# A recurrent attention with an MoE layer: wide products on four tiles, turns by transposes, slabs of two chunks, and an order that counts TensorE's recent use

## The chip, the cores and the metric

The kernel runs on one core of one Trainium2 chip. The core has five engines that each work through their own queue of instructions in order: TensorE (PE in the profile, with its weight loads as PEld), VectorE (DVE), ScalarE (ACT), GpSimd (POOL) and SyncE (SP). DMAs are issued from the queues of ScalarE and SyncE. The metric is the device time of one execution in microseconds (us), as a median of several runs.

## The reference

For each of 4 x 8 heads a 40 x 40 state runs over 768 steps, and its output then goes through a layer norm and a two-layer product with a relu.

```python
for t in range(S):
    y[:, :, t] = np.einsum('bhd,bhde->bhe', rt, state)
    Sa = np.einsum('bhde,bhe->bhd', state, at)
    state_decay = state * wt[:, :, None, :] - np.einsum('bhd,bhe->bhde', Sa, bt)
    state = state_decay + np.einsum('bhd,bhe->bhde', vt, kt)
...
xn = (x - mu) / np.sqrt(var + 1e-06) * g_ln
ch = np.maximum(xn @ w_ch1, 0.0) @ w_ch2
return (x + ch).astype(np.float32)
```

x is y with the heads side by side, so 320 wide; w_ch1 is 320 x 1280 and w_ch2 1280 x 320.

## The kernel before

The 768 steps are cut into 24 chunks of 32. Inside a chunk the recurrence becomes products of matrices, for all 32 heads at once, and only the state passes from chunk to chunk. The heads are laid out by four bits: `h2` and `j`, `gg`, and two bits `b`. Sixteen blocks (`P`) lie along the free dimension and two halves of 40 partitions (rows 0 to 39 and 64 to 103; `half`) or four quarters of 32 (`quad`) along the partitions.

What runs for each chunk c:

- `prep`: ScalarE's queue loads w, a and kb. VectorE makes running products of the decay (`g`, L431, and `q`, L440) and GpSimd scales a and kb by them. TensorE then makes the products of kb with a (`pg`, L477, 64 x 32 results), which VectorE multiplies by a mask of signs into `gk`; the transposes `KB` of kb (L498) and `gY` of g (L464). SP stores half of `gk` to DRAM (`dg`).
- `invert`: for a slab of several chunks, SP fetches the 16 x 16 diagonal blocks from DRAM (`yl`), VectorE inverts them in 14 steps of two instructions for the whole slab (L367, tiles `y` and `tmpy`), and SP writes the result to DRAM twice (`td`, L540, and `ta`, L543). `SLABS` lists the slabs: two of two chunks, then five of four.
- `chain`: the part that goes from chunk to chunk. SP loads N, A and T back from DRAM. `j1` and `j2` (L576) complete the inverse. `pra` and `prb` (L550) add, in one PSUM tile, the share of the chunk's own v (`vpart`) and of the state (`spart`). `p3` (L627) makes u, ScalarE copies it into `VU` beside v (L634), `ST` (L649) is the change of the state, and VectorE adds it.
- `post`: `S` (L685) and `uT` (L699) turn the state and u by products with the identity, `pz` (L710) makes scores, VectorE masks them into Z, and `y` (L550) sums Z with KB and r with S.
- `norm` and `moe`: layer norm of the result, its transposes (L844, L846), and for each pair of chunks 20 units of MoE work: ten of eight products of the first layer (`ph`, L883 and L887) and ten of six of the second (`po`, L903), with a relu on ScalarE (L891) and the remainder on VectorE (L894) between.

A product's place in the array follows from the partitions of its operands: rows of the array from where the two inputs lie, columns from where the output lies. In `pg_` and `pz_` the input half and the output half are the same index (`half(h2)` and `half(h2, 64)`), in `s_` and `sp_` they are two different ones.

The order of all queues is fixed when the program is built. `Plan.order` is a simulation in the kernel's own code: each step has an engine, a planned duration, a key (smaller goes first) and what it depends on, and at each moment each engine takes the ready step with the smallest key. Two things concern TensorE. First, the planner keeps a model of its clock: in windows of `WIN` us it adds up planned time times `FILL`, a share of the array that it gives to each kind of step, and the next window is planned at full or half speed by that sum. Second, MoE units fill in: a unit is taken at once where none was for `DENSE` = 2.0 us; otherwise they are held back (`PACE`) if few are left for the work that is to come. Where TensorE has nothing ready between 25 and 500 us of the plan (`WARM`), it gets a step `wz` of two products (L972) of a constant tile, whose result nobody reads. `BASE` holds the first key of each family of steps.

## Time and profile before

| | |
|---|---|
| median of 3 runs | 950.91 us |
| lowest and highest | 950.14 and 967.42 us |
| the profiled execution | 950.51 us, of which its span is 948.8 |
| PE busy, of the span | 816.7 us, 86% |
| PE weight loads busy | 744.9 us |
| DVE, ACT, POOL busy | 344.3, 199.1, 155.7 us |
| mean granted clock of TensorE | 0.723 |
| DMA moved | 73.85 MB |

The span runs from the first instruction to the last; the time of an execution lies 1.7 us above it here. A row of the lines view names a line, an engine, the tiles written and read, and how often the instruction stands; behind the bar are its busy time in us and the mean of one in ns, then the idle time of the engine just before, and what ended it. A row of the timeline has a start and a duration in us. A row of the windows view is a stretch of the span: its length, the busy time of each engine with the number of instructions, the granted clock, the DMA share and the rate in GB/s; for a single line only PE and PEld stand there. A float32 product is two instructions of the trace, so the 32 of a group in the program are 64 in the profile; a transpose and an MoE product are one.

### The profile page before, as it was taken

To read this page: it belongs to the slowest core of one execution; us is meant where nothing else is said; L and a number is where in the kernel's file an instruction comes from. 1 tells how busy PE (TensorE), PEld (TensorE's weight loads), DVE (VectorE), ACT (ScalarE), POOL (GpSimd) and SP (SyncE) were. 2 spreads that over 40 slices of the span, in tenths; PEclk is the share of its full clock that TensorE was granted. 3 is DMA by queue.
4 is the path that set the end of the run, shared out by engine and by line. 5 is a ranking of instruction groups with operands and counts; after the bars stand their busy time and mean duration, and the time that the engine had idled before them with its cause. 6 is when DMAs were issued, how large, how long until landed. Compare 5 with 4: busy or idle time off the path is not lost. (4 is left out here: it accounts for less than half of the span.)

```text
span 948.8 us, 44592 instructions
## 1 busy us (share of the span) xinstructions
PE 816.7 (86%) x20924; PEld 744.9 (79%) x20924; DVE 344.3 (36%) x700; ACT 199.1 (21%) x433; POOL 155.7 (16%) x215
## 2 busy tenths in 40 slices
PE   3779999999698999699999598999688999678997
PEld 3678988988687888588888587888688889577797
DVE  5374234589202238401227511217711225012231
ACT  1042334421111122111212021212112211112211
POOL 4151123363200003300004300003300000000000
PEclk9985556699655569655659776558866969678799
DMA  8764434344412224622133532124332131211000
GB/s 209 182 154 105 114 89 99 95 119 91 106 46 70 47 67 89 134 53 52 42 78 99 107 85 51 44 62 114 69 75 49 44 65 21 63 41 35 18 2 31
DMA packets 164182, 73.85 MB, mean 78 GB/s; under 512 B 131352, under 2 KB 146712, under 8 KB 163992
## 3 DMA queue, kind: packets, MB, share of 16 engines
q10 hardware_dynamic: 59256, 50.22, 21.1%
q1 hardware_dynamic: 104736, 20.72, 11.0%
q8 instruction: 165, 2.70, 1.2%
q14 instruction: 25, 0.20, 0.1%
HBM read 59.64 MB, written 11.27 MB: 75 GB/s over the span
## 5 line engine op out<-in xcount | busy, mean ns | idle before, releaser
L903 PE MATMUL po<-w_f,hh 128*128 128x320 f32 x480 | 135.5, 372 | 1.0 <-issue 1.0
L883 PE MATMUL ph<-xh,w_f 128*128 128x256 f32 x480 | 135.4, 341 | 0.0
L883 PEld LDWEIGHTS ph<-xh,w_f 128*128 128x128 f32 x480 | 99.6, 229 | 4.6 <-issue 1.0
L903 PEld LDWEIGHTS po<-w_f,hh 128*128 128x128 f32 x480 | 93.7, 227 | 4.4 <-issue 1.3
L894 DVE SCALAR_TENSOR_TENSOR hl<-ph,hh 128x512 fp32r<-128x512 f32 x60 | 41.0, 684 | 149.5 <-ACT hh L891 149.5
L903 PE MATMUL po<-w_f,hl 128*128 128x320 f32 x240 | 85.2, 355 | 0.8 <-DVE hl L894 0.8
L710 PEld LDWEIGHTS att<-r,vt 40*64 40x64 f32 x1536 | 75.3, 200 | 6.7 <-issue 5.6
L367 POOL TENSOR_TENSOR a<-a,g 104x512 f32<-104x512 f32 x24 | 31.6, 1316 | 298.4 <-DVE g L431 177.9
L710 PE MATMUL att<-r,vt 40*64 40x32 f32 x1536 | 78.6, 274 | 2.2 <-issue 2.2
L883 PE MATMUL ph<-xl,w_f 128*128 128x256 f32 x240 | 77.3, 322 | 0.0
L477 PE MATMUL att<-a,kb 40*64 40x32 f32 x1536 | 57.4, 235 | 16.8 <-POOL kb L367 8.1
L972 PE MATMUL po<-warm 128*128 128x192 f32 x346 | 71.2, 372 | 0.0
L477 PEld LDWEIGHTS att<-a,kb 40*64 40x64 f32 x1536 | 54.7, 153 | 20.5 <-POOL kb L367 9.3
L972 PEld LDWEIGHTS po<-warm 128*128 128x128 f32 x346 | 63.5, 277 | 2.2
L367 DVE TENSOR_TENSOR Z<-att,mask 128x512 f32<-128x512 f32 x24 | 16.6, 690 | 134.2 <-PE att L710 78.7
L891 ACT ACTIVATE hh<-ph 128x512 fp32r<-128x512 f32 x60 | 35.9, 598 | 124.7 <-PE ph L887 118.6
L576 PE MATMUL att<-A,N 16*32 16x16 f32 x1536 | 25.3, 204 | 42.3 <-DMA A<-d_a 38.3
L367 POOL TENSOR_TENSOR kb<-kb,q 104x1024 f32<-104x1024 f32 x22 | 54.4, 2472 | 25.8 <-issue 19.2
L634 ACT COPY VU<-att 32x320 f32<-32x320 f32 x96 | 40.0, 417 | 85.4 <-PE att L627 81.0
L576 PEld LDWEIGHTS att<-A,N 16*32 16x32 f32 x1536 | 22.9, 141 | 43.6 <-DMA A<-d_a 31.6
L903 PEld LDWEIGHTS po<-w_f,hl 128*128 128x128 f32 x240 | 54.9, 229 | 2.4 <-DVE hl L894 1.3
L865 POOL TENSOR_SCALAR sm<-mv 128x2 f32<-128x2 f32 x12 | 4.7, 388 | 316.6 <-DVE mv L837 316.5
(114 smaller groups left out, 1334.7 us busy)
## 6 DMA issues: line engine op xcount, KB each, us to landing
w<-in_w_dram ACTq DMA_DIRECT2D x24, 416.0 KB
kb<-in_kb_dram ACTq DMA_DIRECT2D x24, 416.0 KB
a<-in_a_dram ACTq DMA_DIRECT2D x24, 208.0 KB
r<-in_r_dram ACTq DMA_DIRECT2D x24, 208.0 KB
vt<-in_dv_dram ACTq DMA_DIRECT2D x24, 208.0 KB
VU<-in_vt_dram ACTq DMA_DIRECT2D x48, 80.0 KB
VS<-in_vs_dram ACTq DMA_DIRECT2D x48, 80.0 KB
out_dram<-ot SPq DMA_DIRECT2D x24, 160.0 KB
```

Of the source, the lines that this page charges most:

```text
L367: eng.tensor_tensor(out=out, in0=a, in1=b, op=op)
L477: M.matmul(banks(o)[half(h2, 64), b // 2, C * (4 * (b % 2) + 2 * gg + j):C * (4 * (b % 2) + 2 * gg + j) + C], lhsT=kb[half(h2), 2 * (4 * j ...
L576: M.matmul(bank(o)[quad(b), 16 * x:16 * x + 16], lhsT=lhsT[quad(b, n), x], rhs=rhs(b, x), start=True, stop=True, skip_group_check=True)
L634: lambda o, qs=qs, gg=gg, cb=cb, p3=p3: COPY(out=VU[qs].rearrange("p (x y n) d -> p x y n d", x=2, y=2)[:, :, cb], in_=banks(p3)[qs, :, 0: ...
L710: M.matmul(bank(o)[half(gg, 64), C * x:C * x + C], lhsT=flat(vt.rearrange("p n x t -> p n (x t)"))[half(gg), 64 * x:64 * x + 64], rhs=r[ha ...
L865: G.tensor_scalar(out=sm[:, 2], in0=mv[:, :, 1], scalar1=1e-6, scalar2=None, op0=ALU.add)
L883: M.matmul(pv, lhsT=l, rhs=r[:, k], start=n == 0, stop=False, skip_group_check=True)
L891: A.activation(out=hh, in_=ph, func=AF.Relu)
L894: V.scalar_tensor_tensor(out=hl, in0=ph, scalar=0.0, in1=hh.bitcast(F32), op0=ALU.max, op1=ALU.subtract)
L903: M.matmul(po[u][:, 0:CH], lhsT=l[:, us], rhs=wt[:, y], start=f == 0 and n == 0, stop=f == 9 and n == 2, skip_group_check=True)
L972: M.matmul(po_t[0][:, CH:512], lhsT=warm_t[:, 0:128], rhs=warm_t, start=False, stop=True, skip_group_check=True)
```

## The change

Five things change.

1. `pg_` and `pz_` give the output half and the input half different indices, so that a chunk's 32 products use all four combinations. Where results lie in PSUM changes with it: `gk` becomes [128, 4, 4, 32], its sign product two instructions, Z becomes [128, 2, 8, 32], and r and dv are laid out otherwise by the host.
2. `S` and `uT` become transposes of two neighbouring blocks at once: 16 instead of 32 products in the program. For that the blocks of `VU` and `ST` are padded from 40 to 64 columns, and GpSimd clears the four tiles once.
3. `vpart` reads v from `VU`; the tile `VS` and its two loads a chunk go. Its products are split in two by whether their input rows and their bank go together. Between the halves a new step `fence` writes one element of each bank on VectorE. y is split likewise: half of r with S (`ys`), a fence, Z with KB and the other half of r with S (`yz`).
4. All slabs have two chunks.
5. The planner counts use: `used(t)` is planned clock times fill over the last `WIN` us. Where it is below `LOW` = 0.46, TensorE takes an MoE unit if one is ready, otherwise a step `wz`, now a single product of 512 columns into a free ph tile. `DENSE` and `PACE` go. Keys in `BASE`, several planned durations and `FILL` change.

```diff
-SLABS = [[0, 1], [2, 3]] + [list(range(i, i + 4)) for i in range(4, NCH, 4)]
+SLABS = [[i, i + 1] for i in range(0, NCH, 2)]
...
-BASE = dict(chain=-100.0, post=-60.0, prep=-70.0, inv=-45.0, load=-90.0, moe=400.0, wts=-20.0)
+BASE = dict(chain=-48.0, post=-64.0, prep=-66.0, inv=-53.0, load=-90.0, moe=94.0, wts=-20.0)
...
-WIN, DENSE, PACE = 3.413, 2.0, 0.7
-WARM = 25.0, 500.0
+WIN, LOW, WARM = 3.413, 0.46, 20.0
...
+        def used(t):
+
+            while hist and hist[0][1] <= t - WIN:
+                hist.pop(0)
+            return sum((b - max(a, t - WIN)) * f for a, b, f in hist) / WIN
...
-                        if now and t - dense > DENSE:
+                    if e == "PE" and t >= WARM and moes and used(t) < LOW:
...
+        for n in range(RING["VU"]):
+            add("zVU", "POOL", 0.2, lambda o, n=n: G.memset(VU_t[n], 0.0), -890, writes=[("zVU", n)])
...
-                        M.matmul(banks(o)[half(h2, 64), b // 2, C * (4 * (b % 2) + 2 * gg + j):C * (4 * (b % 2) + 2 * gg + j) + C],
+                        M.matmul(banks(o)[half(gg, 64), h2, C * bj:C * bj + C],
                                  lhsT=kb[half(h2), 2 * (4 * j + b) + gg],
...
+    def fence(name, first, key):
+
+        add(name, "DVE", 0.1, lambda o: V.memset(banks(first)[0:1, :, 511:512], 0.0), key, frm=first)
...
-            add(f"ld_s{c}_{gg}", "ACT", 0, lambda o, gg=gg: A.dma_start(
-                out=flat(VS)[quad(2 * gg)], in_=vs_in[c, gg]), kl, writes=[("VS", c, gg)], nbytes=82000)
...
+        def vpart(t, same):
+            for j in range(2):
+                for b in range(4):
+                    for gg in range(2):
+                        h2 = gg if same else 1 - gg
+                        n, y = 8 * (b % 2) + 4 * (b // 2) + 2 * h2 + j, 2 * j + gg
+                        acc_mm(t[quad(b), h2, D * y:D * y + D], seen, (b, h2), gk[quad(2 * gg), b, 2 * h2 + j],
+                               VU[quad(2 * gg), n, 0:D])
...
+        fence(f"prf{c}", pr, k - .1)
+
+        def prb(o):
+            vpart(banks(pr), True)
+            if c:
+                spart(banks(pr))
...
-                            M.matmul(banks(o)[half(gg), h2, D * jb:D * jb + D], lhsT=ST[half(h2), 8 * gg + 2 * b + j],
-                                     rhs=ident[half(h2), half(h2)], start=True, stop=True, skip_group_check=True)
+                        M.transpose(out=banks(o)[0:104, h2, D * gb:D * gb + D],
+                                    in_=flat(ST)[half(h2), 128 * gb:128 * gb + 104],
+                                    identity=ident[half(h2), half(h2)])
...
-                    M.matmul(bank(o)[half(gg, 64), C * x:C * x + C],
-                             lhsT=flat(vt.rearrange("p n x t -> p n (x t)"))[half(gg), 64 * x:64 * x + 64],
-                             rhs=r[half(gg), x], start=True, stop=True, skip_group_check=True)
+                        M.matmul(banks(o)[half(gg, 64), j, C * bh:C * bh + C], lhsT=flat(vt.rearrange("p n x t -> p n (x t)"))[half(j), 64 * n:64 * n + 64],
+                                 rhs=r[half(j), n], start=True, stop=True, skip_group_check=True)
...
+            py = add(f"ys{c}", "PE", 0.28, lambda o: ys(()), k + .45, reads=[("r", c), ("S", c)], nb=2, mode=(64, 32))
+            fence(f"yf{c}", py, k + .55)
...
-        for n in range(2):
-            M.matmul(po_t[0][:, CH:512], lhsT=warm_t[:, 0:128], rhs=warm_t, start=False, stop=True,
-                     skip_group_check=True)
+        w = fin["w1_0_0"] if o.late[1] else hh_t[0]
+        M.matmul(ph_t[o.late[0]], lhsT=w[:, 0:128], rhs=w, start=True, stop=True, skip_group_check=True)
```

Counted over the whole program, the steps `wz` are 346 products before and 74 after, and the fences 47. What that makes of the order is shown at three places. In the rows, "x32" is the number of equal instructions of the program in a row, att are the two PSUM tiles of the attention, and the numbers behind a name tell buffers apart.

The first place is TensorE's queue early on, where the first two chunks are worked through. Before:

```order
L649 MATMUL att_69<-VU_117,KB_105 40x40 x32
L710 MATMUL att_70<-r_122,vt_120 64x32 x32
L699 MATMUL att_70<-ident,VU_117 40x32 x32
L972 MATMUL po_73<-warm 128x192 x10
L550 MATMUL att_69<-VS_118,gk_100 32x40 x32
L550 MATMUL att_69<-ST_135,a_89 32x40 x32
L550 MATMUL att_70<-KB_104,Z_138 32x40 x32
L972 MATMUL po_73<-warm 128x192 x2
L685 MATMUL att_69<-ident,ST_136 40x40 x32
```

And after, at the same steps:

```order
L721 MATMUL att_70<-r_119,vt_117 64x32 x32
L691 MATMUL att_69<-ident,ST_133 104x40 x16
L998 MATMUL ph_71<-hh_155 128x512
L549 MATMUL att_70<-KB_103,Z_135 32x40 x32
L549 MATMUL att_69<-VU_116,gk_98 32x40 x16
L998 MATMUL ph_71<-hh_155 128x512
L474 MATMUL att_70<-a_90,kb_92 64x32 x32
L549 MATMUL att_69<-VU_116,gk_98 32x40 x16
L549 MATMUL att_69<-ST_133,a_87 32x40 x32
```

The turn of the state is 16 instructions of 104 columns instead of 32 of 40, the products of gk with v come in two halves of 16 with another group between them, and single wide `wz` products stand where runs of narrow ones did.

The second place is VectorE's queue near the end of the inversion of the second slab. Before:

```order
L367 TENSOR_TENSOR tmpy<-y_133 128x26
L367 TENSOR_TENSOR y_133<-y_133,tmpy 128x13x2
L367 TENSOR_TENSOR tmpy<-y_133 128x14
L367 TENSOR_TENSOR y_133<-y_133,tmpy 128x14
L536 COPY yT_131<-y_133 128x16x16
```

After, at the end of the same inversion:

```order
L360 TENSOR_TENSOR y_130<-y_130,tmpy 128x13x2
L360 TENSOR_TENSOR xt_137<-att_70,pi_109 128x2x4x40
L862 BN_STATS st_147<-xt_137 128x6
L863 BN_AGGR mv_149<-st_147 128x2
L866 TENSOR_SCALAR xc_142<-xt_137,mv_149 128x320
L554 MEMSET att_69 1x2
L360 TENSOR_TENSOR tmpy<-y_130 128x14
L360 TENSOR_TENSOR y_130<-y_130,tmpy 128x14
L535 COPY yT_128<-y_130 128x16x16
```

The fence (L554) stands in the same queue as the steps of the inversion and of the layer norm, and comes when these are done.

The third place is TensorE's queue in the middle of the run, where MoE units and attention groups alternate. Before, one second-layer unit (L903, six products) and what stands around it:

```order
L649 MATMUL att_69<-VU_117,KB_105 40x40 x32
L903 MATMUL po_73<-w_3_f,hh_159 128x320 x2
L903 MATMUL po_73<-w_3_f,hl_161 128x320
L903 MATMUL po_74<-w_3_f,hh_159 128x320 x2
L903 MATMUL po_74<-w_3_f,hl_161 128x320
L576 MATMUL att_70<-T_125,W_130 32x16 x32
L699 MATMUL att_70<-ident,VU_117 40x32 x32
L550 MATMUL att_69<-VS_118,gk_100 32x40 x32
L550 MATMUL att_69<-ST_135,a_89 32x40 x32
```

After, two such units (L929):

```order
L929 MATMUL po_73<-w_6_f,hh_156 128x320 x2
L929 MATMUL po_73<-w_6_f,hl_158 128x320
L929 MATMUL po_74<-w_6_f,hh_156 128x320 x2
L929 MATMUL po_74<-w_6_f,hl_158 128x320
L707 MATMUL att_69<-ident,VU_115 104x32 x16
L657 MATMUL att_70<-VU_115,KB_103 40x40 x32
L929 MATMUL po_73<-w_7_f,hh_156 128x320 x2
L929 MATMUL po_73<-w_7_f,hl_158 128x320
L929 MATMUL po_74<-w_7_f,hh_156 128x320 x2
L929 MATMUL po_74<-w_7_f,hl_158 128x320
L721 MATMUL att_69<-r_119,vt_117 64x32 x32
L549 MATMUL att_70<-VU_116,gk_98 32x40 x16
```

Four attention groups stood between this unit and the next; now it is two.

## The prediction

> **What bounds the kernel now.** I read the page's busy rows and its clock row first, then the cores view for the mean granted clock.

> ```profile
> span 948.8 us, 44592 instructions
> PE 816.7 (86%) x20924; PEld 744.9 (79%) x20924; DVE 344.3 (36%) x700; ACT 199.1 (21%) x433; POOL 155.7 (16%) x215
> PEclk9985556699655569655659776558866969678799
> q1 hardware_dynamic: 104736, 20.72, 11.0%
> ```
> ```profile
> core 0: 948.8 us, clock 0.723
> ```

> TensorE is busy 86% of the span and nothing else reaches 40%, so TensorE sets the time. But its clock is granted at 0.723 on average. It has two values here, 0.50 and 1.00, so (1 - 0.723) / 0.5 = 55% of the span, 526 us, ran at half. The windows view says where.

> ```profile
> 75.00:100.00 25.00, 24.52 (x520) 22.91 (x522) 9.75 (x32) 5.52 (x13) 3.22 (x4) 0.50 0.44 107
> 300.00:325.00 25.00, 23.75 (x736) 20.71 (x738) 5.35 (x10) 4.74 (x10) 0.40 (x1) 0.50 0.19 45
> 400.00:425.00 25.00, 23.08 (x689) 21.01 (x684) 1.51 (x2) 5.52 (x15) 1.28 (x1) 0.50 0.25 64
> ```
> ```profile
> 300.00:325.00 25.00, 0.00 (x0) 0.00 (x0) 0.50 0.19 45
> 400.00:425.00 25.00, 5.90 (x18) 4.70 (x18) 0.50 0.25 64
> 650.00:675.00 25.00, 7.14 (x44) 6.59 (x45) 1.00 0.43 102
> ```

> The first fence is all of TensorE: busy 23 to 24.5 of 25 us, and yet at half clock. The second is the second-layer MoE products alone (L903): none in 300 to 325, 18 in 400 to 425 (half clock both times), 44 in 650 to 675, where the clock is full throughout. So "busy" is not what earns the clock. The small attention products fill little of the array; the clock comes with MoE products standing close together. In the three half-clock rows PE is busy 71.35 of 75 us, 95%, so about 526 x 0.95 = 500 of the 817 busy us, 61%, ran at half. What the half clock costs, and what the changed products cost, is in the timeline and the lines view (duration is the second column of the timeline, busy total the first number after the bar of a line).

> ```profile
> 324.82 3.63 PE L710 MATMUL att<-r,vt 40*64 40x32 f32 x64
> 736.67 2.06 PE L710 MATMUL att<-r,vt 40*64 40x32 f32 x64
> 284.47 2.34 PE L699 MATMUL att<-ident,VU 32*40 32x32 f32 x64
> 750.12 1.41 PE L699 MATMUL att<-ident,VU 32*40 32x32 f32 x64
> 739.79 0.83 PE L649 MATMUL att<-VU,KB 64*40 64x40 f32 x64
> 524.57 0.69 PE L498 MATMUL att<-ident,kb 40*128 40x40 f32 x16 [1.22 <-DVE gk L367]
> ```
> ```profile
> L710 PE MATMUL att<-r,vt 40*64 40x32 f32 x1536 | 78.6, 274 | 2.2 <-issue 2.2
> L972 PE MATMUL po<-warm 128*128 128x192 f32 x346 | 71.2, 372 | 0.0
> L477 PE MATMUL att<-a,kb 40*64 40x32 f32 x1536 | 57.4, 235 | 16.8 <-POOL kb L367 8.1 <-DMA d_g<-gk 4.7 <-POOL rec L367 3.4
> L699 PE MATMUL att<-ident,VU 32*40 32x32 f32 x1536 | 47.3, 227 | 2.1 <-issue 1.8 <-ACT xh L850 0.2
> L685 PE MATMUL att<-ident,ST 40*40 40x40 f32 x1472 | 27.8, 243 | 5.7 <-issue 5.7
> L498 PE MATMUL att<-ident,kb 40*128 40x40 f32 x384 | 19.3, 254 | 3.3 <-DVE gk L367 3.3
> ```

> The same 64 products take 3.63 us at half and 2.06 at full, 2.34 and 1.41: a us of half-clock work costs 0.57 to 0.60 us at full, so 0.40 of it can be won.

> **The sum, against the profiled execution** (950.51 us: span 948.8 and 1.7 around it; the median of the runs shown, 950.91, is 0.4 above). Of the span PE works 816.7 and is idle 132.1.

> *Wide products on four tiles (pg, L477; pz, L710).* Before, row half and column half are always equal, so two of the four 64x64 tiles work. L649 has the same 64 instructions on all four tiles and takes 0.83, where L699, on two, takes 1.41: a factor of 0.59, although each L649 streams 40 columns instead of 32. Ends: a factor of 1 (64-column weight loads don't overlap) and 0.50. I take 0.55, next to the measured 0.59: 0.45 x (78.6 + 57.4) = 61 us off; ends 0 and 68.

> *State and u by transposes.* Two-pass products with the identity become one-pass transposes, two blocks at a time: 64 instructions become 16, of the shape that L498 has, 19.3 / 24 = 0.80 us a chunk at this clock mix. L699: 47.3 - 19.3 = 28 off. L685: 27.8 - 23 x 0.80 = 9 off. Ends: 0.69 each (all at full) and about 1.1 (all at half): 31 to 43 in sum, 37 taken.

> *Warm-up products.* 346 of 192 columns, 71.2 us, become 74 of 512. At 71.2 / 66,432 columns x 37,888 columns that is 41 us; at full clock, by the L710 ratio, some 0.7 of that or less. They stand almost all ahead of the first MoE product, where TensorE waits for loads anyway. I take 24, so 47 off; ends 30 and 55.

> *Split accumulations.* The prediction product (pra, prb) and y each get one or two more switches between groups: some 0.1 us, three a chunk, 7 us more (0 to 15).

> At an unchanged clock, PE work is 816.7 - 61 - 37 - 47 + 7 = 679.

> *The order.* I laid full-clock durations of such rows on the two orders, from the first MoE product to the last. Before, 189 of 312 us of attention products stand in stretches over 2.5 us without a MoE product, the longest 6.6; after, 80 of 262, the longest 3.7. That is 61% and 31%. Before, 61% of PE's busy time is at half. I let the half share follow the stretches: of 679 us, 414 at half becomes 210, and 204 us turned to full win 0.40 x 204 = 82. This is the weakest step. Its ends: nothing won, and all 414 turned, 166. PE work: 597.

> *Slabs of two.* Each slab's inverse goes through SP's queue.

> ```profile
> 49.97 2.08 SPq L540 DMA_DIRECT2D d_t<-y  x4
> 52.14 2.03 SPq L543 DMA_DIRECT2D d_a<-yT  x4
> 64.18 0.73 PE L576 MATMUL att<-A,N 16*32 16x16 f32 x64
> 376.48 4.13 SPq L540 DMA_DIRECT2D d_t<-y  x8
> 380.71 5.34 SPq L543 DMA_DIRECT2D d_a<-yT  x8
> 395.18 1.05 PE L576 MATMUL att<-A,N 16*32 16x16 f32 x64 [6.93 <-DMA A<-d_a]
> ```
> ```profile
> PE att L576 <- DMA A<-d_a: 38.3, 5, 9.0
> ```
> ```profile
> L367 DVE TENSOR_TENSOR tmpy<-y 128x28 f32<-128x28 f32 (+13 forms) x98 | 28.5, 291 | 24.5 <-DMA y<-d_g 17.0 <-issue 4.6
> L367 DVE TENSOR_TENSOR y<-y,tmpy 128x28 f32<-128x28 f32 (+13 forms) x98 | 24.8, 253 | 3.4
> L431 DVE TENSOR_TENSOR_SCAN g<-w,start 104x512 f32<-104x512 f32 x24 | 32.8, 1368 | 2.1 <-POOL rec L367 0.8 <-PE att L464 0.6
> ```

> From the first store to the first product that needs it: 14.2 us for two chunks, 18.7 for four. SP issues 8 stores instead of 16 before a load can go. Four-chunk slabs stalled PE five times, 38.3 us. Twelve slabs now; the faster TensorE reaches the product sooner, the chain is shorter. I take 2.5 us each, 30 us; ends 0 and 12 x 7.7 = 92. VectorE gets 336 steps for 196; at 0.19 to 0.29 each that is some 25 us more, the split sign product some 5: 375 of 740 us, no bound. SP gets no more issues per chunk.

> *Fences.* 47 one-element writes on VectorE stand between two halves of an accumulation: TensorE's second half, and all behind it in its queue, waits for VectorE to reach them. In the order one group (0.4 to 2 us) mostly stands between the halves and covers a free VectorE. Ends: 0, and 47 x 1.37 behind a scan each, 64. I take 0.3 each, 14, because VectorE is busy half the time.

> *Loads.* The vs loads go (48 of 80 KB). The VU loads come in pieces of 160 bytes, 24,576 packets more; by the q1 row, the queue with the small packets, one takes 0.11 x 16 x 948.8 / 104,736 us = 16 ns, so 25 us on each of 16 engines: hidden. Four POOL memsets stand ahead of chunk 0's product, 0 to 5 us once; taken as 0.

> Idle: 132.1 - 38.3 + 30 + 14 = 138. Time: 597 + 138 + 1.7 = 737 us.

> [...] In the trace, identity transposes (L498) run in stretches that also hold MoE products, so no row tells what they earn alone. [...]

> **Rivals.**
> 1. *Full clock from the first MoE product on.* For it: the row 650 to 675, and the even order. Against it: the order is fixed, and the row 400 to 425 shows interleaved MoE products at half clock. 679 - 166 + 125 idle + 2 = 640.
> 2. *The clock mix stays.* Once at half, interleaved work does not lift it (400 to 425), and any stall of 7 us that the plan didn't foresee drops it. 679 + 138 + 2 = 819.
> 3. *Transposes earn no clock.* If each of 47 groups costs one more window of 3.4 us at half: 47 x 3.4 x 0.40 = 64 on top of 737: 801.
> 4. *The waits grow.* Fences behind a scan each (64) and stalls of 7.7 in every slab (92): 737 + 50 + 62 = 849.
> 5. *Slower.* With MoE products spread evenly and few dense runs left, TensorE falls to half after the first stall and stays there: the 265 us at full become 265 / 0.6 = 442, 414 + 442 + 140 = 996. It decides only where the granted clock stays under about 0.53; 300 to 425 shows that it can for 100 us, the dense runs speak against it.

> **How the numbers follow.** The forecast, the clock partly won, 680 to 790: 0.55. Rival 1: 0.13; 2: 0.15; 3: 0.08; 4: 0.06; 5: 0.03. Predicted 737. Low 640 is rival 1, high 840 takes in 2, 3 and most of 4. Faster by over 2% (about what a measurement of this kernel can tell from no change, 19 us) are all but rival 5, less a little for what I don't see: 0.95; within 2%: 0.02; slower: 0.03.

> **What would show it.** L477 and L710's successors at about 1.1 us for 64 at full clock, not 2; the transposes x16 at 0.7. Mean granted clock about 0.83 (0.72 is rival 2, over 0.95 rival 1, under 0.55 rival 5). Waits for d_a under 3 us each in twelve slabs; waits of TensorE for the one-element writes under 0.5 us each. I would be wrong if the four-tile groups stay near 2 us, or if the clock falls where transposes gather.

## The result, and the profile after

The changed kernel takes 819.1 us (median of four runs, 807.56 to 827.53) against 954.92 us before on the same chip. The ratio, 0.853 with a 95% interval from 0.836 to 0.869, is not the quotient of these medians, because it and the ratios further down leave out the runs that fell in a second, slower state. The new kernel is faster, and the time lies in the predicted range, but 82 us above the predicted 737. It is the time of the second rival, in which the clock mix stays.

The page of the new kernel and its cores view; the profiled execution took 827.53 us, the longest of the four, and the sums below are made against it:

```profile
span 825.8 us, 39753 instructions
...
PE 704.4 (85%) x18396; PEld 615.4 (75%) x18396; DVE 362.8 (44%) x915; ACT 199.4 (24%) x433; POOL 156.0 (19%) x219
...
PEclk9975555875559655777595756795755768887899
...
q8 instruction: 145, 2.38, 1.2%
```
```profile
core 0: 825.8 us, clock 0.716
```

TensorE works 112 us less, but at the same clock: 0.716 is (1 - 0.716) / 0.5 = 57% of the span at half, 469 us, where it was 55% before. The lines view shows that the edited products did what was expected of them:

```profile
L474 PE MATMUL att<-a,kb 40*64 40x32 f32 x1536 | 39.7, 265 | 20.6 <-issue 12.6 <-POOL a L360 5.6 <-ACT pi L463 2.4
L721 PE MATMUL att<-r,vt 40*64 40x32 f32 x1536 | 36.5, 255 | 0.0
L998 PE MATMUL ph<-hh 128*128 128x512 f32 x64 | 32.8, 641 | 0.0
L691 PE MATMUL att<-ident,ST 40*104 40x40 f32 x368 | 18.9, 267 | 2.4 <-issue 2.4
L707 PE MATMUL att<-ident,VU 32*104 32x32 f32 x384 | 18.9, 250 | 0.0
```

The timeline (start, duration) has a four-tile group at half and at full clock, and the transposes of u:

```profile
96.80 1.91 PE L721 MATMUL att<-r,vt 40*64 40x32 f32 x64
649.98 1.14 PE L721 MATMUL att<-r,vt 40*64 40x32 f32 x64
94.88 0.90 PE L707 MATMUL att<-ident,VU 32*104 32x32 f32 x16
```

Where the clock was not won shows best in work that the change leaves alone. The windows view for a single line counts overlapping rows once; over the whole span, first before (L903, L883, L887), then after (L929, L909, L913), the MoE products:

```profile
0.00:949.00 949.00, 154.97 (x720) 130.14 (x720) 0.72 0.33 78
0.00:949.00 949.00, 136.19 (x720) 114.88 (x720) 0.72 0.33 78
0.00:949.00 949.00, 55.78 (x240) 45.30 (x240) 0.72 0.33 78
```
```profile
0.00:826.00 826.00, 166.50 (x720) 138.57 (x720) 0.72 0.37 84
0.00:826.00 826.00, 145.32 (x720) 123.22 (x720) 0.72 0.37 84
0.00:826.00 826.00, 58.12 (x240) 47.75 (x240) 0.72 0.37 84
```

The same 1,680 products cost 346.9 us before and 369.9 after. Spread evenly, they run at half clock more often, not less: by the clock rows of the traces 490 of them began at half before, and 675 after.

The windows view of the new kernel around two waits (length, then busy time of PE, PEld, DVE, ACT, POOL with counts, granted clock, DMA share, GB/s) shows how a stretch at half begins:

```profile
455.50:462.00 6.50, 5.85 (x311) 5.17 (x308) 5.94 (x7) 1.18 (x2) 3.33 (x4) 1.00 0.56 131
462.00:465.40 3.40, 1.11 (x124) 0.99 (x108) 0.00 (x0) 0.44 (x1) 0.00 (x0) 1.00 0.71 133
465.60:485.80 20.20, 20.20 (x521) 17.77 (x522) 5.54 (x12) 4.82 (x11) 0.00 (x0) 0.50 0.23 56
```
```profile
544.20:557.50 13.30, 13.30 (x254) 12.14 (x253) 11.20 (x30) 3.48 (x7) 3.68 (x3) 1.00 0.37 66
557.50:560.90 3.40, 0.74 (x52) 0.63 (x44) 1.85 (x5) 0.20 (x1) 3.07 (x7) 1.00 0.42 98
561.10:588.20 27.10, 23.15 (x529) 21.38 (x530) 12.89 (x37) 5.10 (x12) 6.93 (x8) 0.50 0.37 88
```

One stretch of 3.4 us in which TensorE works 1.11 or 0.74 us was enough here; behind it the clock stays at half for 20 and 27 us, in the first case with TensorE busy 20.20 of 20.20. In the clock rows of this trace every stretch at half is a multiple of 3.41 us long, from 3.41 to 88.75, but the last, which runs to the end of the span. The two waits end in these rows of the timeline, where the bracket has the idle time before the row and what ended it:

```profile
464.56 0.70 PE L549 MATMUL att<-KB,Z 64*32 64x40 f32 x56 [2.29 <-issue]
565.05 1.05 PE L578 MATMUL att<-A,N 16*32 16x16 f32 x64 [6.80 <-DMA A<-d_a]
```

The second is for the slab's inverse. The first is of a kind that I had passed over, in the middle of a group:

```profile
509.67 0.75 PE L549 MATMUL att<-ST,a 40*32 40x40 f32 x62
...
510.25 0.60 PE L549 MATMUL att<-KB,Z 64*32 64x40 f32 x43
512.88 0.30 PE L549 MATMUL att<-KB,Z 64*32 64x40 f32 x17 [2.03 <-issue]
```

This is another one of that kind, at 510. Of 64 identical products TensorE has done 45, stands for 2.03 us, and goes on; nothing that the profile shows released it ("issue"). The waits view sums them:

```profile
PE att L549 <- issue: 28.0, 18, 2.6
PE att L578 <- DMA A<-d_a: 26.3, 6, 6.8
...
PE att L549 <- DVE att L554: 1.6, 2, 1.0
```

In the trace, 23 stops of more than 0.8 us lie inside a group, 37.4 us in all. Counted in TensorE's records (a weight load or a matmul), they lie a multiple of 256 apart, but for about one record in each 256, and each has a 16 KB packet of the queue named instruction within 2 us of its start. That queue's row agrees: 2.38 MB in 145 packets are 16.4 KB each, and 2 x 18,396 records over 145 packets are 254 a packet. So I read the stops as TensorE's own code arriving late; no row shows that directly. The packets are never less than 3.3 us apart here, and small products can pass their records faster than that: in the first two rows of the timeline at 510, 105 matmuls with as many loads, 210 records, pass in 1.2 us. Before the change there were such stops too (21, 33 us).

The trace's clock rows show what stood before each fall of the clock. In the new kernel it falls 22 times, always behind a 3.4 us stretch in which TensorE worked 2.73 us or less, though a few with 2.2 to 2.7 us passed without a fall. The longest idle time in that stretch was a wait for d_a in five cases, a stop inside a group in 13 and another wait in four. The stretches at half that followed sum to 113, 195 and 160 us; 89 of the last are a single stretch near the start, from 52 us on.

### The profile page after: what moved, and what is told of

Same layout as the page of the kernel before. It is cut to its first block, busy times and chain, and to the rows that moved or that the text cites. A ratio compares the mean times of both kernels' runs of the same rounds, so it can differ in the third digit from the quotient of the medians.

```text
span 825.8 us, 39753 instructions
## 1 busy us (share of the span) xinstructions
PE 704.4 (85%) x18396; PEld 615.4 (75%) x18396; DVE 362.8 (44%) x915; ACT 199.4 (24%) x433; POOL 156.0 (19%) x219
## 3 DMA queue, kind: packets, MB, share of 16 engines
q1 hardware_dynamic: 104736, 20.72, 12.8%
q8 instruction: 145, 2.38, 1.2%
## 5 line engine op out<-in xcount | busy, mean ns | idle before, releaser
L929 PE MATMUL po<-w_f,hh 128*128 128x320 f32 x480 | 145.2, 395 | 2.3 <-issue 1.6
L909 PE MATMUL ph<-xh,w_f 128*128 128x256 f32 x480 | 144.2, 358 | 0.4 <-DVE hl L920 0.4
L909 PEld LDWEIGHTS ph<-xh,w_f 128*128 128x128 f32 x480 | 106.6, 245 | 5.6 <-issue 0.7
L929 PEld LDWEIGHTS po<-w_f,hh 128*128 128x128 f32 x480 | 99.7, 241 | 9.3 <-issue 4.1
L929 PE MATMUL po<-w_f,hl 128*128 128x320 f32 x240 | 89.2, 372 | 0.6 <-issue 0.5
L909 PE MATMUL ph<-xl,w_f 128*128 128x256 f32 x240 | 80.9, 337 | 0.0
L360 POOL TENSOR_TENSOR a<-a,g 104x512 f32<-104x512 f32 x24 | 31.6, 1316 | 191.9 <-DVE g L428 181.3
L909 PEld LDWEIGHTS ph<-xl,w_f 128*128 128x128 f32 x240 | 59.8, 249 | 0.1
L929 PEld LDWEIGHTS po<-w_f,hl 128*128 128x128 f32 x240 | 58.6, 244 | 0.4 <-DVE hl L920 0.4
L474 PE MATMUL att<-a,kb 40*64 40x32 f32 x1536 | 39.7, 265 | 20.6 <-issue 12.6
L474 PEld LDWEIGHTS att<-a,kb 40*64 40x64 f32 x1536 | 36.6, 188 | 24.5 <-issue 15.1
L578 PE MATMUL att<-A,N 16*32 16x16 f32 x1536 | 24.4, 203 | 35.5 <-DMA A<-d_a 26.3
L360 DVE TENSOR_TENSOR tmpy<-y 128x14 f32<-128x14 f32 (+6 forms) x168 | 38.1, 227 | 34.0 <-DMA y<-d_g 23.8
L428 DVE TENSOR_TENSOR_SCAN g<-w,start 104x512 f32<-104x512 f32 x24 | 32.2, 1343 | 21.3 <-issue 11.7
L360 DVE TENSOR_TENSOR xl<-att,xh 128x384 fp32r<-128x384 f32 x24 | 13.4, 556 | 61.2 <-ACT xh L876 42.9
L360 DVE TENSOR_TENSOR ST<-att,ST 104x640 f32<-104x640 f32 x22 | 18.1, 823 | 49.6 <-PE att L657 49.6
```

What stands on the lines that cost most here:

```text
L360: eng.tensor_tensor(out=out, in0=a, in1=b, op=op)
L428: add(f"g{c}", "DVE", 1.3, lambda o: V.tensor_tensor_scan(out=flat(g), data0=w[:, 0], data1=flat(start0), initial=0.0, op0=ALU.mult, op1=A ...
L474: M.matmul(banks(o)[half(gg, 64), h2, C * bj:C * bj + C], lhsT=kb[half(h2), 2 * (4 * j + b) + gg], rhs=a[half(h2), 8 * gg + 4 * j + b], st ...
L578: M.matmul(bank(o)[quad(b), 16 * x:16 * x + 16], lhsT=lhsT[quad(b, n), x], rhs=rhs(b, x), start=True, stop=True, skip_group_check=True)
L909: M.matmul(pv, lhsT=l, rhs=r[:, k], start=n == 0, stop=False, skip_group_check=True)
L929: M.matmul(po[u][:, 0:CH], lhsT=l[:, us], rhs=wt[:, y], start=f == 0 and n == 0, stop=f == 9 and n == 2, skip_group_check=True)
```

## The experiments

Four theories were set against each other. A: the plan's fills count use that the array doesn't have. B: waits that the plan doesn't know of drop the clock. C: the earlier rule's dense runs of MoE units are what lifts it. D: small products run into the code's arrival. All runs start from the new kernel; times are medians, clock, PE and idle time those of the profiled execution. That is one of four to six, and can be the shortest of them or the longest; where it matters, the clocks of the others are given.

| run | us | ratio to before, 95% | clock | PE busy | idle |
|---|---|---|---|---|---|
| new kernel | 819.1 | 0.836 to 0.869 | 0.716 | 704.4 | 121.4 |
| fill_refit | 818.3 | 0.851 to 0.865 | 0.737 | 706.9 | 108.1 |
| low_70 | 841.6 | 0.868 to 0.889 | 0.829 | 719.1 | 124.3 |
| order_of_before | 874.5 | 0.905 to 0.924 | 0.728 | 800.5 | 86.2 |
| order_of_before_cold | 886.7 | 0.916 to 0.930 | 0.720 | 717.3 | 165.5 |
| slabs_of_four | 841.2 | 0.874 to 0.889 | 0.735 | 701.6 | 143.7 |
| turns_as_products | 862.8 | 0.886 to 0.902 | 0.720 | 722.7 | 140.4 |
| two_tiles_at_a_time | 838.7 | 0.867 to 0.879 | 0.739 | 724.2 | 103.9 |
| unit_every_160 | 808.9 | 0.833 to 0.847 | 0.747 | 683.8 | 121.2 |
| plan_slow_stores | 777.4 | none given | 0.776 | 675.0 | 97.1 |
| plan_slow_stores_160 | 733.3 | 0.754 to 0.772 | 0.815 | 642.4 | 90.7 |
| plan_slow_stores_160_refit | 746.3 | 0.762 to 0.783 | 0.815 | 661.6 | 83.0 |
| no_late_warm | 740.6 | 0.766 to 0.778 | 0.771 | 663.5 | 87.6 |

### Other fills

```diff
-FILL = dict(gY=.46, KB=.46, pg=.47, pra=.69, prb=.66, ... S=.42, uT=.35, ...
+FILL = dict(gY=.25, KB=.25, pg=.47, pra=.10, prb=.20, ... S=.25, uT=.25, ...
```

> Only the planner's table of fills is changed: the transposes (KB, gY, S, uT) from .46, .46, .42, .35 to .25, pra from .69 to .10 and prb from .66 to .20, values fitted to which 3.4 us windows of the profile before were followed by a full clock. The plan gets 114 warm products instead of 74 and MoE units earlier. Theory A (the plan counts use that the array doesn't have, so its order lets the clock fall): mean granted clock up from .72 to .78 or more, time 750 to 790. Theory B (the clock falls because TensorE waits 1 to 4 us in places where the plan has no wait, whatever the fills): clock .70 to .74, time 805 to 835. Theory C (dense runs of MoE units, which the earlier rule made and the new one doesn't, are what lifts the clock): as B.

818.3 us, the new kernel's time, at a clock of 0.737 where A expected 0.78. A falls in this form.

### More filling

```diff
-WIN, LOW, WARM = 3.413, 0.46, 20.0
+WIN, LOW, WARM = 3.413, .70, 20.0
```

> LOW goes from 0.46 to 0.70, nothing else: 369 warm products of 512 columns instead of 74, and MoE units taken as soon as they are ready. 295 more warm products at the .23 to .45 us that 512 columns take cost 68 to 130 us of TensorE. Theory A: clock over .85, and the gain at 429 us of half-clock work pays for them: 780 to 830. Theory B: the more even filling covers some waits; clock .75 to .80, 830 to 880. Theory C: clock near .72, 880 to 950.

The clock comes, the time doesn't: 841.6 us is in B's range, the clock above it, and no case fits in both. From the lines view of this run:

```profile
L998 PE MATMUL ph<-w_f 128*128 128x512 f32 x219 | 84.8, 517 | 0.0
...
L998 PE MATMUL ph<-hh 128*128 128x512 f32 x150 | 57.1, 531 | 0.0
```

The warm products take 141.9 us, 102 more than in the new kernel. All other PE work is 577 us against 665: 88 us won for 0.113 of clock. My price, 0.40 us for each us turned from half to full, gives 0.113 / 0.5 x 843 x 0.40 = 76. So the price of the clock was about right.

### The earlier order

The planner, keys, fills and warm products of the kernel before (`DENSE`, `PACE`, `BASE`, `order`), and in a second run also

```diff
-WARM = 25.0, 500.0
+WARM = 25.0, 110.0
```

> The products, transposes, fences and slabs of the new kernel with the planner, keys, fills and warm products of the kernel before (DENSE 2.0, PACE 0.7). Theory C: the dense runs come back, clock .76 or more, time 740 to 790. Theories A and B: the new order is no worse than the old one at the same waits; clock .70 to .73, time 815 to 860, the upper part for the 425 warm steps.

> As order_of_before, but warm steps only up to 110 us of the plan instead of 500. That run had 157 us of warm products against 40 in the new kernel, and its time was 55 us longer. If the new order's gain is only that it leaves out warm products: 800 to 835 at a clock of .70 to .73. If the even order itself is worth something: 840 to 870. If the dense runs of the earlier rule lift the clock when no warm products stand beside them (theory C): under 800, clock over .75.

874.5 and 886.7 us, clock 0.728 and 0.720. The profiled execution of the first is its longest; its other three have 0.749 to 0.767, more than the new kernel's four (0.716 to 0.748). But that run has 157 us of warm products. Without most of them the clock is 0.714 to 0.722 in all four executions, where C expected over 0.75. So C falls: the earlier order by itself has no better clock. The new order is worth 55 to 68 us here, in the second comparison not through the clock. Without most of the warm products waits come in their place, as the waits view of the second run shows.

```profile
PE att L585 <- DMA A<-d_a: 45.8, 9, 13.2
...
PE att L556 <- DVE att L561: 9.5, 5, 5.9
```

Which of the keys or rules does it was not taken apart.

### Slabs of four

```diff
-SLABS = [[i, i + 1] for i in range(0, NCH, 2)]
+SLABS = [[0, 1], [2, 3]] + [list(range(i, i + 4)) for i in range(4, NCH, 4)]
```

> Slabs as before (two of two chunks, five of four), all else as in the new kernel. My sum had the slabs of two at 8 us of idle less. If the stalls of TensorE for d_a are what drops the clock (theory B), four-chunk slabs stall longer, waits for d_a over 38 us, clock under .71, time 825 to 860. If slabs don't matter (A, C): 805 to 830.

841.2 us, 22 more. The waits for d_a are 34.3 us instead of 26.3, other idle time 14 more; the clock doesn't fall with them (0.720 to 0.735 in five executions), which theory B had expected. But this plan has 143 warm products where the new kernel's has 74, 77 us against 40, and they may have held it. So the run doesn't decide on B.

### Transposes undone

```diff
-                        M.transpose(out=banks(o)[0:104, gg, x:x + C], in_=flat(VU)[qs, 64 * n:64 * n + 104],
-                                    identity=ident[qs, qs])
+                        for j in range(2):
+                            M.matmul(banks(o)[half(j), gg, x:x + C], lhsT=VU[qs, n + j, 0:D], rhs=ident[qs, qs],
+                                     start=True, stop=True, skip_group_check=True)
```
and S in the same way.

> S and uT are again products with the identity (64 instructions each in the profile, on all four tiles) in place of 16 transposes each, all else and the order as in the new kernel. The traces so far show TensorE stopping in the middle of a group for 1 to 2.6 us, each time where about 256 more of its records (a weight load and a matmul are two) have gone by and within 0.6 us of a 16 KB packet of the queue named instruction, whose packets are never closer than 3.4 us. Theory D (code for small products arrives too slowly): 192 records a chunk more, 17 more packets, so besides some 15 us of work (L657 has 1.1 us for such a group, the transposes .8) up to 60 us of such stops: 845 to 880. Transposes earn no clock (my rival 3): the clock rises above .74 and the time falls, 780 to 815. Neither: 825 to 845.

862.8 us, 44 more, in D's range. Its page:

```profile
PE 722.7 (84%) x20652; PEld 632.0 (73%) x20652; DVE 359.4 (42%) x915; ACT 199.7 (23%) x433; POOL 153.5 (18%) x219
...
q8 instruction: 163, 2.67, 1.3%
```

4,512 more records are 18 more packets. PE works 18 us longer, as the rows say, and the stops inside groups grow from 37.4 us (23) to 58.3 us (36), 21 us more, about the 19 us that idle time grows. The time and the stops are as D expected. The clock, 0.720, is what it was. Rival 3 was an assumption that no row of the kernel before spoke for, and this run shows no sign of it: products in the place of the 24 and 23 groups of transposes earned no more clock (0.720 against 0.716).

### Two tiles at a time

```diff
-            for bh in range(8):
-                for gg in range(2):
-                    for j in range(2):
+            for x in range(2):
+                for bh in range(8):
+                    for gg in range(2):
+                        j = gg ^ x
```
and pg in the same way.

> pg and pz with the same products, but written so that 16 products whose row half equals their column half come first and 16 others behind, so that only two of the four tiles can work at one time. My sum had four tiles at 61 us less: the two rows back to 130 us or more, time 870 to 890. If the four tiles don't overlap and the gain came from elsewhere: 815 to 830. If the longer groups let the code arrive in time (theory D) some of the 61 us is won back: 850 to 870.

838.7 us, between the expected cases. The rows of pg and pz are 63.1 and 58.6 us, 45.5 more than the 76.2 on four tiles, so products on the four combinations of halves do overlap. But PE as a whole works only 20 us longer, and the median is 20 us longer. In the profile the clock is 0.739 and idle time 17 us less; that is the shortest execution of this run beside the longest of the new kernel, and over all four the clocks (0.725 to 0.739, against 0.716 to 0.748) don't differ clearly. The stops inside groups, 34 us (22) against 37 (23), hardly change, so little of it is fewer stops. Why shorter groups don't give their whole time back stays open.

### A unit every 160 records

```diff
-                    if e == "PE" and t >= WARM and moes and used(t) < LOW:
+                    if e == "PE" and t >= WARM and moes and (used(t) < LOW or sent >= EVERY):
...
+                        sent = 0 if o.moe is not None else sent + RECS.get(o.name.rstrip("0123456789_"), 2)
```

> The planner takes a MoE unit also where 160 records of small products have gone by since the last one (a unit is 12 or 16 records that take about 1 us at full clock), not only where the counted use is under 0.46; no warm products for that reason. Theory D: the stops in the middle of groups of small products, 37 us in 23 places in the new kernel, fall under 20 us, and as the clock fell right behind such stops, it rises to .75 or more: 770 to 800. If the stops are only a symptom: 810 to 835. Theory A or C: 805 to 830.

808.9 us, less than expected of D: stops inside groups 30 us (20), not under 20, clock 0.747. The interval of its ratio overlaps the new kernel's, so the 10 us are not clear of noise.

### The plan learns how slow SyncE's queue is

```diff
-                        free[e] = t + 0.06
+                        free[e] = t + (0.6 if e == 'SP' else 0.06)
...
-                        end = max(t + 2.0, dma_free[q] + 1.2)
+                        end = max(t + 5.5, dma_free[q] + 3) if q == 'SP' else max(t + 2.0, dma_free[q] + 1.2)
```

> Only what the planner believes of SyncE's queue is changed: an issue keeps SP for 0.6 us instead of 0.06, and a DMA of SP's lands 5.5 us after it, or 3 us behind the queue, instead of 2.0 and 1.2. In the new kernel's profile the way from the first store of a slab (L539, 372.94) to the product that needs it (388.1) is 15 us, which the plan takes to be much shorter, so it puts j1 too early. Theory B (unplanned waits let the clock fall): the waits for d_a go from 26 us to under 8, the clock rises to .75 or more behind them, time 750 to 785. If only the waits go: 795 to 805. If other waits come in their place (theory D, the code): 805 to 830.

> plan_slow_stores and unit_every_160 together. If the two causes add up: 20 to 40 us under the better of the two alone, clock .80 or more, 715 to 765. If the second takes nothing more: within 10 us of plan_slow_stores.

> The same, and with the lower fills of fill_refit (KB, gY, S, uT .25, pra .10, prb .20, and values for j and p3, whose names never matched the table). Theory A in its second form (fills matter once the waits are in the plan): clock .82 or more at 100 to 160 warm products, 700 to 755. If fills don't matter: within 10 us of plan_slow_stores_160.

777.4 us with these two lines alone, 733.3 with the rule of 160 records beside them: 86 us under the new kernel, with the same products but for 18 and 35 more warm ones. The waits view of the first and the cores view of the second:

```profile
PE att L549 <- issue: 33.6, 24, 2.6
...
PE att L578 <- DMA A<-d_a: 2.7, 1, 2.7
```
```profile
core 0: 733.1 us, clock 0.815
```

The waits for d_a go from 26.3 to 2.7 us and the clock rises by 0.06 (0.741 to 0.776 in four executions, against 0.716 to 0.748), with time and clock in the ranges that B named. The stops inside groups remain; with MoE units between the small products the clock rises to 0.815, and the MoE products fall from 369.9 us (new kernel) over 354.0 to 329.2. The rule that won 10 us alone wins 44 here.

The clock rows show that it isn't simply a matter of fewer falls. In plan_slow_stores the clock falls 23 times against 22, none of them behind a wait for d_a and 18 behind a stop inside a group; but the stretches at half sum to 345 us instead of 468. With the rule of 160 it falls 19 times, for 270 us. So what the first change won is shorter stretches, and why they are shorter is not shown.

The lower fills on top give 746.3 us, inside the range of A's second form, but 13 us above the same kernel without them, at the same clock of 0.815 and with 19 us more of warm products. They win nothing.

### No warm products behind the first unit

```diff
-                            if x is not None:
+                            if x is not None and not held:
```

> plan_slow_stores_160 without the warm products behind the first MoE unit (24 rows of ph<-w_f, 12.9 us in its profile; 85 before the first unit stay). If they earn nothing any more, now that the waits are in the plan: 8 to 13 us less, 718 to 728, clock .80 to .83. If they hold the clock where no unit is ready: clock under .80, 735 to 760.

740.6 us (734.59 to 752.86) against 733.3 (726.97 to 737.85): no gain, though 12.9 us of TensorE's work are gone, so these warm products cost nothing in sum. Whether they pay in clock is not clear: the profiled execution (0.771) is the longest, and the other five have 0.788 to 0.816, against 0.807 to 0.839 with them.

## Why the prediction held in its range and missed its point

Term by term, against the profiled execution (704.4 + 121.4 + 1.7 = 827.5):

| term of the sum | predicted | measured |
|---|---|---|
| pg and pz on four tiles | -61 | -59.8 |
| state and u by transposes | -37 | -37.3 |
| warm-up products | -47 | -31.6 |
| split accumulations (pra, prb and y) | +7 | -12.9 (91.6 to 78.7 us) |
| the clock won by the order | -82 | none; the MoE products +23.0 |
| waits for d_a | -8 | -12.0 |
| fences | +14 | 1.6 us of waits shown |
| idle time in all | 138 | 121.4 |

- The edits to products were priced right from the neighbouring rows: the factor of 0.55 for four tiles (measured 0.56), 0.8 us for 16 transposes. (The low end of 31 us for the transposes is a slip: at 1.1 us each they would win 23.)
- Warm-ups were 15 us too cheap: 64 of them stand in the head, where one takes 0.64 us on average. By the trace it is 0.72 us for the 31 at half and 0.41 for the 11 at full; the 22 ahead of the first clock row take 0.65. I had priced them near full clock.
- The split accumulations were taken as a cost, at an estimated 0.1 us a switch that no row gave, and are a gain: 78.7 us instead of 91.6. The groups now run through one kind of operand at a time; that this is the reason was not tried.
- **The step that failed is the order**: "I let the half share follow the stretches", 82 us, which the prediction called its weakest. It rested on one agreement, 61% on both sides before. After the change the stretches without a MoE product are 31% and the half share is 57% of the span. These stretches were measured in planned time. On the chip, waits of 1 to 7 us stand in them: the slab's inverse, which the plan expects too early, the stops inside groups of small products, of which it knows nothing, and a few others. Before each of the 22 falls a 3.4 us stretch held 2.73 us of work or less, and evenly spread units then took 3.4 to 51 us to raise the clock, over 20 us in eight of the 21 cases behind the first, which took 89 near the start. With the first wait in the plan and MoE units placed against the second, the clock is 0.815 and the time 733, near the forecast's 0.83 and 737. That comes from a plan that the change didn't have, and the parts differ: PE works 642 us and is idle for 91, where the forecast had 597 and 138. The nearness of the times is luck.
- Rival 2 gave 819 and came nearest to the trace ("any stall of 7 us that the plan didn't foresee drops it"; one of 6.80 us stands at a fall here, and stops of up to 2.6 us inside groups stand at others). Its parts were less exact than its sum: PE 679 against 704.4, idle 138 against 121.4, errors that cancel, and the profiled execution is 8 us longer than the median.
- Idle time was predicted for the right total of d_a waits (30, measured 26.3) with the wrong shape: six waits are shown, up to 6.8 us, not twelve under 3. Slabs of two are worth 22 us, warm products included, where my sum had 8 on idle time.

How much of the clock each kind of wait costs is not separated: plan_slow_stores also moves other work, and no run took the stops inside groups away. The count of falls says only what stood before each.

## What to carry to other kernels

An order written out in advance is only as good as the latencies in it: measure the slow queue's way from store to use in a profile (15 us here) and put that in the plan (777.4 us instead of 819.1), before tuning fills or thresholds. Where a share of useful work has to hold the clock, leave no stretch as long as the 3.4 us seen here to luck; evenly spread work took up to 51 us here to win a lost clock back. Count instructions as well as their time: where a TensorE group of many small products is followed by another, put a few long products between them (44 us here, but only with the waits in the plan), or use fewer instructions (4,512 records more brought 21 us of stops).
